# Seven accumulator banks as one set, freed in the order of their last readers, and two alternating orders of the attention step

## The chip, the cores and the metric

The kernel runs on one core of a Trainium2 chip. TensorE (PE) multiplies matrices and writes its results into PSUM, which has eight banks of 128 partitions by 512 fp32 values. VectorE (DVE), ScalarE (ACT) and GpSimd (POOL) do the rest; SyncE (SP) issues the transfers. Each engine takes its own instructions strictly in their order and waits on semaphores of the others. The metric is the device time of one launch in microseconds; lower is better.

## The reference

A transformer block on 2048 rows of 448 values, all in fp32: layer norm, attention with 16 heads of 28 values that share one key and one value head, output projection and residual; then layer norm, a gated feed-forward part of width 1792, and residual.

```python
q = (x @ wq).reshape(B, S, H, Dh).transpose(0, 2, 1, 3);  k = x @ wk;  v = x @ wv      # x = layernorm(A_x)
scores = jnp.einsum("bhqd,bkd->bhqk", q, k) * (Dh ** -0.5)
o = jnp.einsum("bhqk,bkd->bhqd", softmax(scores), v)
h = A_x + o.transpose(0, 2, 1, 3).reshape(B, S, H * Dh) @ wo
z = layernorm(h)
out = h + (silu(z @ w1) * (z @ w3)) @ w2
```

## The kernel before, in words

The rows are cut into four tiles of 512 (`t`), the heads into four groups of four (`g`). A **block** `i = 4t + g` is one tile with one group, so there are 16 blocks. Values that need fp32 precision are split into a high and a low part, and products are made of two or three fast passes.

**Opening stage.** Layer norm of all rows, transposes (`ln_tr`, L161), keys and values (`kv`, L405), queries of all blocks (`q`, L424). Between these the row maxima of block 0 and of the first quarter of block 1 are made in pairs (`both`, L231, called by `pairs`, L439).

**Attention stage.** Of each block the row maximum of all scores comes first, since the exponent must not overflow. It takes 64 **units** (`Unit`, L211): one matmul of 128 queries against 512 keys (L224) into a bank, and one maximum over 512 values on VectorE (`red`, L229). The exponents take 16 **steps** per block, one for each 128 keys (`c`): four **heads** (`Head`, L260), each of two accumulating matmuls (L271) into a bank and one Exp on ScalarE (L277), which writes to SBUF; then `pv` (L279), four matmuls side by side that add the step before to the output bank `po`. Step `s = 16 i + c`, 256 in all. The units run 20 steps ahead of the heads, four units in each of the first 236 steps (`a_units`, L337); the last 20 steps have heads alone.

Scores use half of the PE array's rows (64), so two matmuls on the two halves run side by side. I call such a couple a **slot**. A step of before is: heads 0 and 1 side by side (two slots); head 2 beside units u0 and u1 (two slots); `pv` of the step before; head 3 beside units u2 and u3 (two slots). This order is written out by hand in the loop from L547, the same for each step; `todo` (L505) adds other work at places `s + 0.4` (before the first two maxima), `s + 0.5` (after them, ahead of `pv`) and `s` (at the step's end).

That other work: at step 16i - 5 of block i the maxima are joined (`max_done`, L238); at step 16i - 3 they are transposed into a bank (`max_rows`, L242: PE L245, ScalarE copy L247) and their low part is made on VectorE (`max_low`, L250: L252), and eight small transfers on SP's queue (L258) put both parts into the rows that heads of block i use. Heads 0 and 1 of the block's first step need the fifth and the seventh of these. The output projection (`wo_rows`, L314) stands at the end of 12 even steps, the normalisation (`ln_norm`, L152) at the end of 8 odd steps, and the transposes for the feed-forward part (`ln_tr`) in 8 odd steps.

**Feed-forward stage.** For each tile 14 chunks of the width: `ffn1` (L594) makes two banks of 22 matmuls in all, `ffn2` (L606) adds 12 matmuls to four banks that stay taken for the whole tile.

**The banks.** Three banks (`ps_a`, tiles `pa`) serve the units, the projection and `ffn1`; four (`ps_b`, tiles `pb`) serve heads, queries, transposes and the feed-forward sums; one is `po`. Each set is handed out in a ring: a new tile takes the bank of the tile three (four) before it in the same set, and its first matmul waits until that tile's reader is done. In the heads-only steps one of the four heads uses a bank of `ps_a`.

Of the kernel before, what the change touches and what calls it, by code (L numbers as in the profile page):

```python
# [35 lines left out]
def block_kernel(  # L36
# [27 lines left out]
    dr_pool = ctx.enter_context(tc.tile_pool(name="dr", bufs=2, space=DRAM))  # L64
    ps_a = ctx.enter_context(tc.tile_pool(name="ps_a", bufs=3, space=PSUM))
    ps_b = ctx.enter_context(tc.tile_pool(name="ps_b", bufs=4, space=PSUM))
    ps_o = ctx.enter_context(tc.tile_pool(name="ps_o", bufs=1, space=PSUM))
# [30 lines left out]
    def put_late():  # L98
        for k in range(2):
            put_w13(10 + 2 * k, keep.tile([P, NG, T], F32, name=f"w13_{k}", tag=f"os{k}"))  # L100
            tl = keep.tile([P, NG, D], F32, name=f"w2_wo{k}", tag=f"wo{k}")
            for g in range(NG):
                W2[8 + 4 * k + g] = tl[:, g]


# [54 lines left out]

    def ln_tr(t, c, ps, spare=False):  # L161
        if c == 0:
            XT[t] = (xt_pool.tile([P, 4, T], F32R, name="xh"), xt_pool.tile([P, 3, T], F32R, name="xl"))
        xh, xl = XT[t]
        xns = LN[t][3]
        for n in range(NQ):
            pe.transpose(ps[:, n * P : (n + 1) * P], xns[n][:, c * P : (c + 1) * P], ident)  # L167
        se.activation(xh[:, c], ps, AF.Copy)
        eng = ve
        if spare:  # L170
            x32 = wk_pool.tile([P, T], F32, name="rb")
            se.activation(x32, ps, AF.Copy)
            eng, ps = ge, x32
        if c < 3:
            eng.tensor_tensor(xl[:, c], ps, f(xh[:, c]), op=ALU.subtract)  # L175
        else:
            eng.tensor_tensor(xh[64:128, 3], ps[64:128], f(xh[64:128, 3]), op=ALU.subtract)


    def a_bank():  # L180
        return ps_a.tile([P, T], F32, name="pa")

    def b_bank():
        return ps_b.tile([P, T], F32, name="pb")

# [25 lines left out]
    class Unit:  # L211
# [6 lines left out]

        def mm(self, bank=a_bank):
            i, n, kt, r = self.i, self.n, self.kt, rows(self.jj)  # L220
            if i not in MX:
                MX[i] = wk_pool.tile([P, 16, 4], F32, name="mx")
            self.ps = bank()
            pe.matmul(self.ps, QS[i][r, 2 * self.p, n * P : (n + 1) * P], KS[r, kt * T : (kt + 1) * T],  # L224
                      start=True, stop=True)

        def red(self):
            c = 8 * self.jj + 4 * self.p + self.n
            ve.tensor_reduce(MX[self.i][:, c, self.kt : self.kt + 1], self.ps, axis=AX.X, op=ALU.max)  # L229

    def both(i, p, n, kt, bank):  # L231
        us = [Unit(i, p, n, kt, jj) for jj in range(2)]
        for u in us:
            u.mm(bank)
        for u in us:
            u.red()
# [5 lines left out]
    def max_rows(i):  # L242

        ps = b_bank()
        pe.transpose(ps[:16, :P], NM[i], ident)  # L245
        mr = wk_pool.tile([16, 2, P], F32R, name="mr")
        se.activation(mr[:, 0], ps[:16, :P], AF.Copy)  # L247
        MR[i] = ps, mr

    def max_low(i):  # L250
        ps, mr = MR.pop(i)
        ve.tensor_tensor(mr[:, 1], ps[:16, :P], f(mr[:, 0]), op=ALU.subtract)  # L252
        for k in range(2):
            for jj in range(2):
                r = 64 * jj + 32 * k + 28
                for p in range(2):
                    c = 8 * jj + 4 * p
                    sy.dma_start(f(QS[i][r : r + 1, 2 * p]).rearrange("o (n q) -> o n q", n=NQ), f(mr[c : c + 4, k]))  # L258

    class Head:  # L260


        def __init__(self, i, c, j, bank=b_bank):
            self.i, self.c, self.j, self.bank = i, c, j, bank

        def mm(self, k):
            i, c, (p, jj) = self.i, self.c, divmod(self.j, 2)
            if k == 0:
                self.ps = self.bank()
            r = rows(jj)  # L270
            pe.matmul(self.ps, KS[r, c * P : (c + 1) * P], QS[i][r, 2 * p + k], start=(k == 0), stop=(k == 1))  # L271

        def exp(self):
            i, c, (p, jj) = self.i, self.c, divmod(self.j, 2)
            if jj == 0:
                PT[i, c, p] = p_pool.tile([P, 2, T], F32R, name="pt")
            se.activation(f(PT[i, c, p][:, jj]), self.ps, AF.Exp, bias=0.0, scale=SCALE)  # L277

    def pv(i, c):  # L279
# [33 lines left out]

    def wo_rows(t, n, bank=a_bank):  # L314
        ps = bank()[:, :D]
        k = 0
        for a, b in ((0, 0), (1, 0), (0, 1)):
            for g in range(NG):
                pe.matmul(ps, OS[a][:, g, n * P : (n + 1) * P], WO[b][:, g],  # L319
                          start=(k == 0), stop=(k == 11))  # L320
                k += 1
        ve.tensor_tensor(X[t][:, n], ps, X[t][:, n], op=ALU.add)

    def split_w(k):
# [12 lines left out]
    def a_units(step):  # L337
# [4 lines left out]
        p, n = divmod(c // 2, NQ)  # L342
        return [Unit(i, p, n, 2 * (c % 2) + k, jj) for jj in (1, 0) for k in range(2)]

# [6 lines left out]
    with tc.tile_pool(name="start", bufs=1) as sp:  # L351
# [49 lines left out]
        def tr(t, *cs):  # L401
            for c in cs or range(4):
                ln_tr(t, c, b_bank())

        def kv(t, between=None):  # L405
            cols = slice(t * T, (t + 1) * T)
            ps = b_bank()
            mm_D(ps[:96], WKV, XT[t], slice(0, 96), slice(0, T), between)
# [4 lines left out]
            sy.dma_start(f(KS[64:128, cols]), f(KS[0:64, cols]))  # L413
            sy.dma_start(f(KS[28::32, cols]), ones)
            return vt

        def va(t, vt):
            ps = b_bank()
            for n in range(NQ):
                pe.transpose(ps[:, 32 * n : 32 * n + 32], vt[64:96, n * P : (n + 1) * P], ident[64:96, 64:96])  # L420
            ve.tensor_copy(VA[:, NQ * t : NQ * t + NQ, :DH],
                           ps[:, :P].rearrange("p (n r) -> p n r", n=NQ)[:, :, :DH])

        def q(t, g, between=None):  # L424
            ps = b_bank()
            mm_D(ps, [w[:, :, 4 * g : 4 * g + 4].rearrange("p c h r -> p c (h r)") for w in WQ],
# [3 lines left out]
            else:  # L430
                se.activation(QR[t][:, g], ps, AF.Copy)

        first = [(both, 0, *divmod(pn, NQ), kt) for kt in range(4) for pn in range(8)]
# [5 lines left out]
        def pairs(n=2):  # L439
            banks = [a_bank, b_bank] * n  # L440
            while n > 0 and first:
                fn, *args = first.pop(0)
                if fn is both:
                    fn(*args, banks.pop(0))
                    n -= 1
                else:
                    fn(*args)

# [75 lines left out]
    for t in range(NT - 1):  # L524
# [9 lines left out]
        for c in range(4):  # L534
            at(e + 33.5 + 2 * c, lambda t, c: ln_tr(t, c, b_bank(), True), t, c)
    for t in range(NT):
# [10 lines left out]
    for s in range(LAST):  # L547
# [4 lines left out]
        if s == LAST - 2:  # L552
            WS[0, 0] = split_w2(0)
        hs = [Head(i, c, j, b_bank if au or j < 3 else a_bank) for j in range(4)]
        for k in range(2):
            for h in hs[:2]:
                h.mm(k)
        for h in hs[:2]:
            h.exp()
        if au:  # L560
            for j in (2, 3):
                for k in range(2):
                    hs[j].mm(k)
                    au[2 * (j - 2) + k].mm()
                hs[j].exp()
                if j == 2:
                    run(s + 0.4)
                for u in au[2 * (j - 2) : 2 * (j - 2) + 2]:
                    u.red()
                if j == 2:  # L570
                    run(s + 0.5)
                    if prev is not None:
                        pv(*prev)
        else:
            for k in range(2):
                for h in hs[2:]:
                    h.mm(k)
            for h in hs[2:]:
                h.exp()
            run(s + 0.4)  # L580
# [13 lines left out]
    def ffn1(t, k, W):  # L594
        ps = [a_bank(), a_bank()]
        for m in range(2):
            mm_D(ps[m], [w[:, :, m] for w in W], XT[t], slice(0, P), slice(0, T))
        sg = f(p_pool.tile([P, 2, T], F32R, name="pt")[:, 0])
        se.activation(sg, ps[0], AF.Silu)  # L599
        ve.tensor_tensor(sg, ps[1], sg, op=ALU.mult)  # L600
        h = p_pool.tile([P, 2, T], F32R, name="pt")
        se.activation(h[:, 0], sg, AF.Copy)  # L602
# [3 lines left out]
    def ffn2(t, k, n):  # L606
        if n == 0 and k == 0:
            Y[t] = [b_bank() for _ in range(NQ)]
        hid, w2s = HID[t, k], WS[t, k]
# [4 lines left out]
    def y_out(t, n):  # L614
        ve.tensor_tensor(X[t][:, n], Y[t][n][:, :D], X[t][:, n], op=ALU.add)
        if t == NT - 1:
            sy.dma_start(ov[t][:, n], X[t][:, n])
# [20 lines left out]
    for t in (NT - 2, NT - 1):  # L638
        for n in range(NQ):
            on(t - 1, 1 + n, ln_norm, t, n)  # L640
        for c in range(4):
            on(t - 1, 5 + c, lambda t, c: ln_tr(t, c, a_bank()), t, c)

# [58 lines left out]
```

## Time and profile before

| what | us |
|---|---|
| median of 3 runs (1276.83 to 1280.04) | 1278.54 |
| the profiled execution | 1276.48 |
| its span, first to last instruction | 1274.7 |
| opening stage | 0 to about 104 |
| attention, steps with units | about 104 to 787 |
| attention, heads-only steps | to about 834 |
| feed-forward | about 834 to 1275 |

The profile's page gives each engine's busy time, the chain of work that ended last, and groups of instructions by line. In the timeline, a row is a run of like instructions: start, length, engine, line, operation, tiles, count, and in brackets how long the engine was idle before and what ended that. A matmul's length includes its way through the array, so two matmuls in a row overlap and their starts tell more than their lengths; PEld is the loading of weights ahead of a matmul.

### The profile page before, as it was taken

What the parts mean: (1) busy time and instruction counts of PE and PEld (TensorE: products, weight loads), DVE (VectorE), ACT (ScalarE), POOL (GpSimd) and SP (SyncE); (2) the same over time, 40 slices, a digit from 0 to 9 for tenths busy, and PEclk for the clock granted to TensorE, in tenths of its full rate; (3) what the DMA queues carried; (4) which work ended last, traced back from release to release, by engine and by line L of the source; (5) the groups of instructions that cost most, each with busy time, mean ns of one, the idle gap of its engine ahead of it and who ended that gap; (6) DMA issues with size and microseconds to landing.
All of it is one profiled execution on the core that took longest, in us unless ns stands there. A gap on an engine that the chain in (4) does not pass through costs nothing.

```text
span 1274.7 us, 19969 instructions
## 1 busy us (share of the span) xinstructions
PE 1257.3 (99%) x7596; PEld 800.2 (63%) x7596; DVE 860.1 (67%) x1480; ACT 664.0 (52%) x1255; POOL 324.3 (25%) x240
## 2 busy tenths in 40 slices
PE   6999999999999999999999999999999999999998
PEld 5655555545555455555555544378888888888887
DVE  7998999999798998898998896033433324333223
ACT  3316777787578877678777678931111211211111
POOL 3201011101102100112100101253456455545551
PEclk9999999999999999999999999999999999999999
DMA  6220103101103111103110101022100000000000
GB/s 186 60 45 2 35 32 76 43 10 35 43 2 75 43 22 23 43 2 75 43 33 12 42 2 43 10 78 80 30 1 30 1 1 30 1 1 30 1 1 29
DMA packets 37960, 43.08 MB, mean 34 GB/s; under 512 B 12056, under 2 KB 30680, under 8 KB 37864
## 3 DMA queue, kind: packets, MB, share of 16 engines
q1 hardware_dynamic: 37864, 41.81, 12.7%
q8 instruction: 60, 0.98, 0.3%
q14 instruction: 36, 0.29, 0.1%
HBM read 20.25 MB, written 3.80 MB: 19 GB/s over the span
## 4 chain that ended last, share of the span: by engine, by line
PE 96%; DVE 2%; issue 1%; POOL 0%; ACT 0%; DMA 0%; SPq 0%; ACTq 0%; POOLq 0%
PE pb L271 27%; PE pa L116 23%; PE po L283 20%; PE pb L611 11%; PE pa L224 8%; PE pb L116 4%; PE pa L319 3%; PE pb L167 1%; DVE mx L229 1%; PE pa L167 0%; DVE xl L175 0%; PE pb L245 0%; PE pb L224 0%; DVE xn L155 0%; DMA X<-in_A_x_dram 0%
## 5 line engine op out<-in xcount | busy, mean ns | idle before, releaser
L229 DVE TENSOR_REDUCE mx<-pa 128x1 f32<-128x512 f32 x998 | 621.5, 682 | 58.7 <-PE pb L271 32.2
L277 ACT ACTIVATE pt<-pb 128x512 f32<-128x512 f32 x1004 | 527.1, 598 | 169.8 <-PE pb L271 138.4
L271 PEld LDWEIGHTS pb<-qs,KS 64*128 64x128 f32 x2008 | 257.7, 184 | 256.6 <-issue 198.0
L271 PE MATMUL pb<-qs,KS 64*128 64x512 f32 x2008 | 417.1, 406 | 1.6 <-issue 0.8
L224 PE MATMUL pa<-KS,qs 64*128 64x512 f32 x998 | 368.8, 445 | 0.8 <-DVE mx L229 0.7
L283 PE MATMUL po<-pt,VA 128*32 128x512 f32 x2048 | 273.5, 605 | 0.0
L116 PE MATMUL pa<-xh,qs 128*128 128x512 f32 x896 | 235.9, 394 | 0.0
L116 PEld LDWEIGHTS pa<-xh,qs 128*128 128x128 f32 x896 | 167.6, 187 | 38.9 <-issue 0.8
L600 DVE TENSOR_TENSOR pt<-pa,pt 128x512 f32<-128x512 f32 x56 | 38.7, 692 | 223.3 <-PE pa L116 223.3
L224 PEld LDWEIGHTS pa<-KS,qs 64*128 64x128 f32 x998 | 162.9, 184 | 37.1 <-DVE mx L229 9.7
L611 PE MATMUL pb<-qst,pt 128*128 128x448 f32 x672 | 145.8, 366 | 0.0
L599 ACT ACTIVATE pt<-pa 128x512 f32<-128x512 f32 x56 | 33.5, 598 | 197.5 <-PE pa L116 197.5
L611 PEld LDWEIGHTS pb<-qst,pt 128*128 128x128 f32 x672 | 125.5, 188 | 12.7
L602 ACT ACTIVATE pt<-pt 128x512 fp32r<-128x512 f32 x56 | 35.4, 632 | 152.8 <-DVE pt L600 152.8
L195 POOL TENSOR_TENSOR qst<-QR,qst 128x512 fp32r<-128x512 f32 x15 | 19.3, 1285 | 333.1 <-ACT qst L194 332.9
L116 PE MATMUL pa<-xl,qs 128*128 128x512 f32 x336 | 96.4, 394 | 0.0
L283 PEld LDWEIGHTS po<-pt,VA 128*32 128x32 f32 x2048 | 40.7, 108 | 64.1 <-issue 60.7
L328 POOL TENSOR_TENSOR qs<-QR,qs 128x1024 fp32r<-128x1024 f32 x32 | 76.4, 2389 | 15.6 <-DVE qs L327 15.6
L116 PEld LDWEIGHTS pa<-xl,qs 128*128 128x128 f32 x336 | 62.9, 187 | 15.5
L307 POOL TENSOR_TENSOR OT<-OT,rb 128x512 f32<-128x512 f32 x16 | 20.7, 1292 | 201.4 <-DMA rb<-sd 68.5
L603 DVE TENSOR_TENSOR pt<-pt 128x512 fp32r<-128x512 f32 x56 | 40.2, 718 | 39.1 <-ACT pt L602 39.1
L334 POOL TENSOR_TENSOR qst<-w_wo,qst 128x448 fp32r<-128x448 f32 x24 | 35.3, 1469 | 93.9 <-DVE qst L333 93.9
(91 smaller groups left out, 692.8 us busy)
## 6 DMA issues: line engine op xcount, KB each, us to landing
qs<-qst SPq DMA_DIRECT2D x128, 128.0 KB
rb<-sd SPq DMA_DIRECT2D x64, 64.0 KB
QR<-in_B_w_dram SPq DMA_DIRECT2D x16, 192.0 KB
X<-in_A_x_dram SPq DMA_DIRECT2D x3, 896.0 KB
out_dram<-X SPq DMA_DIRECT2D x3, 896.0 KB
qs<-mr SPq DMA_DIRECT2D x128, 2.0 KB
w<-in_B_w_dram SPq DMA_DIRECT2D x8, 192.0 KB
w_wo<-in_B_w_dram SPq DMA_DIRECT2D x6, 224.0 KB
```

Of the source, the lines that this page charges most:

```text
L116: pe.matmul(ps, lhs[b][:, cb, lsl], rhs[a][:, ca, rsl], start=(k == 0), stop=(k == len(terms) - 1),)
L224: pe.matmul(self.ps, QS[i][r, 2 * self.p, n * P : (n + 1) * P], KS[r, kt * T : (kt + 1) * T], start=True, stop=True)
L229: ve.tensor_reduce(MX[self.i][:, c, self.kt : self.kt + 1], self.ps, axis=AX.X, op=ALU.max)
L271: pe.matmul(self.ps, KS[r, c * P : (c + 1) * P], QS[i][r, 2 * p + k], start=(k == 0), stop=(k == 1))
L277: se.activation(f(PT[i, c, p][:, jj]), self.ps, AF.Exp, bias=0.0, scale=SCALE)
L283: pe.matmul(PO[i][32 * j : 32 * j + 32], VA[:, c], f(PT[i, c, j // 2][:, j % 2]), start=(c == 0), stop=(c == NC - 1))
L319: pe.matmul(ps, OS[a][:, g, n * P : (n + 1) * P], WO[b][:, g], start=(k == 0), stop=(k == 11))
L328: ge.tensor_tensor(wl, W13[k], f(wh), op=ALU.subtract)
L600: ve.tensor_tensor(sg, ps[1], sg, op=ALU.mult)
L602: se.activation(h[:, 0], sg, AF.Copy)
L603: ve.tensor_tensor(h[:, 1], sg, f(h[:, 0]), op=ALU.subtract)
L611: pe.matmul(Y[t][n][:, :D], hid[a][:, n * P : (n + 1) * P], w2s[:, b, :D], start=(k == 0 and m == 0), stop=(k == NF - 1 and m == 2))
```

## The change

All seven banks beside `po` become one set. `bank()` hands out the bank that stands first in a list; `done()` puts a bank at the end of the list where its last reader is issued. So the n-th tile takes the bank that was given back as the (n-7)th, whatever kind of tile that was: the first matmul of a unit may now wait for ScalarE, that of a head for VectorE.

The steps with units have two orders. Even steps keep the order above. In odd steps heads 0 and 1 come first, then heads 3 and 2 side by side, then units u0 and u1 side by side in one slot, `pv`, and units u2 and u3 in one slot. (The four units of an odd step are listed anew, so that two that run side by side use different halves of the array.) The number of matmuls, maxima, exponents and transfers stays the same, and so does the place of the other work: `s + 0.4`, `s + 0.5` and `s`. Heads-only steps keep their order.

```diff
-    ps_a = ctx.enter_context(tc.tile_pool(name="ps_a", bufs=3, space=PSUM))
-    ps_b = ctx.enter_context(tc.tile_pool(name="ps_b", bufs=4, space=PSUM))
+    ps_w = ctx.enter_context(tc.tile_pool(name="ps_w", bufs=1, space=PSUM))
...
+    free, used = list(range(7)), {}
+
+    def bank(name="pb"):
+        k = free.pop(0)
+        ps = ps_w.tile([P, T], F32, name=name, tag=f"bank{k}")
+        used[id(ps)] = ps, k
+        return ps
+
+    def done(ps):
+        free.append(used.pop(id(ps))[1])
...
         def red(self):
             c = 8 * self.jj + 4 * self.p + self.n
             ve.tensor_reduce(MX[self.i][:, c, self.kt : self.kt + 1], self.ps, axis=AX.X, op=ALU.max)
+            done(self.ps)
...
             ve.tensor_tensor(mr[:, 1], ps[:16, :P], f(mr[:, 0]), op=ALU.subtract)
+        done(ps)
...
             se.activation(f(PT[i, c, p][:, jj]), self.ps, AF.Exp, bias=0.0, scale=SCALE)
+            done(self.ps)
...
-        return [Unit(i, p, n, 2 * (c % 2) + k, jj) for jj in (1, 0) for k in range(2)]
+        us = [Unit(i, p, n, 2 * (c % 2) + k, jj) for jj in (1, 0) for k in range(2)]
+        return us if c % 2 == 0 else [us[0], us[2], us[3], us[1]]
...
+        def pair(a, b):
+            for k in range(2):
+                a.mm(k)
+                b.mm(k)
+            a.exp()
+            b.exp()
+
+        def beside(h, us):
+            for k in range(2):
                 h.mm(k)
-        for h in hs[:2]:
+                us[k].mm()
             h.exp()
...
+        pair(hs[0], hs[1])
+        if au and c % 2 == 0:
+            beside(hs[2], au[:2])
+            run(s + 0.4)
+            red(au[:2])
+            run(s + 0.5)
+            if prev is not None:
+                pv(*prev)
+            beside(hs[3], au[2:])
+            red(au[2:])
+        elif au:
+            pair(hs[3], hs[2])
+            for u in au[:2]:
+                u.mm()
+            run(s + 0.4)
+            red(au[:2])
+            run(s + 0.5)
+            pv(*prev)
+            for u in au[2:]:
+                u.mm()
+            red(au[2:])
         else:
...
+            pair(hs[2], hs[3])
```

The other users of banks (`ln_tr`, `kv`, `va`, `q`, `both`, `wo_rows`, `ffn1`, `ffn2`, `y_out`) take theirs from `bank()` and give it back with `done()` after their last reader in the same way.

The first place is TensorE's queue in a step with units, in block 4. L271 is a head's matmul (`pb`), L224 a unit's (`pa`), L283 is `pv` (`po`); the words in brackets are the semaphores that it waits on. Before, from head 2's first slot to the last slot of the step:

```order
L271 MATMUL pb_2787<-qs_1621,KS_89 128x512 [waits Activation_49]
L224 MATMUL pa_2789<-KS_89,qs_2214 128x512 [waits DVE_49]
L271 MATMUL pb_2787<-qs_1621,KS_89 128x512
L224 MATMUL pa_2792<-KS_89,qs_2214 128x512 [waits DVE_49]
...
L271 MATMUL pb_2803<-qs_1621,KS_89 128x512
L224 MATMUL pa_2805<-KS_89,qs_2214 128x512 [waits DVE_49]
L271 MATMUL pb_2803<-qs_1621,KS_89 128x512
L224 MATMUL pa_2808<-KS_89,qs_2214 128x512 [waits DVE_49]
```

With the change, an odd step from heads 3 and 2 on (lines are those of the changed file: L280 is a head, L231 a unit, L293 `pv`):

```order
L280 MATMUL pb_3080<-qs_1618,KS_86 128x512 [waits DVE_49]
L280 MATMUL pb_3082<-qs_1618,KS_86 128x512 [waits DVE_49]
L280 MATMUL pb_3080<-qs_1618,KS_86 128x512
L280 MATMUL pb_3082<-qs_1618,KS_86 128x512
L231 MATMUL pa_3089<-KS_86,qs_2211 128x512 [waits Activation_49]
L231 MATMUL pa_3091<-KS_86,qs_2211 128x512 [waits DVE_49]
L293 MATMUL po_2799<-pt_3043,VA_87 32x512 x2
L293 MATMUL po_2799<-pt_3053,VA_87 32x512 x2
L231 MATMUL pa_3099<-KS_86,qs_2211 128x512 [waits DVE_49]
L231 MATMUL pa_3101<-KS_86,qs_2211 128x512 [waits Activation_49]
```

The units of the odd step stand two by two on either side of `pv`, all four heads stand ahead of them, and the waits have changed sides: units wait for ScalarE's semaphore too, heads for VectorE's.

The second place is the odd step 16i - 3 on TensorE's queue, where the maxima of a block are transposed (L253 in the changed file, L245 before):

```order
L231 MATMUL pa_3228<-KS_86,qs_2813 128x512 [waits Activation_49]
L231 MATMUL pa_3230<-KS_86,qs_2813 128x512 [waits DVE_49]
L253 MATMUL pb_3232<-ident_84,nm_3173 16x128 [waits DVE_49]
L293 MATMUL po_2799<-pt_3181,VA_87 32x512 x2
L293 MATMUL po_2799<-pt_3192,VA_87 32x512 x2
L231 MATMUL pa_3251<-KS_86,qs_2813 128x512 [waits Activation_49]
L231 MATMUL pa_3253<-KS_86,qs_2813 128x512 [waits Activation_49]
```

Before, the transpose waited for ScalarE and stood behind four slots (heads 0 and 1, then head 2 with two units); now it waits for VectorE and stands behind five, with all four heads of the step ahead of it. On ScalarE its copy (`mr`) stood behind three exponents of the step and now stands behind four; on VectorE its second reader stands behind the first two maxima, as before.

More of the change, by code (lines that the diff above doesn't have):

```diff
@@ L159, in block_kernel, with ln_tr @@
     XT = {}
-    def ln_tr(t, c, ps, spare=False):
+    def ln_tr(t, c, spare=False):
+        ps = last = bank()
         if c == 0:
@@ L177, in ln_tr @@
             eng.tensor_tensor(xh[64:128, 3], ps[64:128], f(xh[64:128, 3]), op=ALU.subtract)
[L180 to L184, printed above, removed]
+        done(last)
     MR = {}
@@ L217, in __init__, with mm @@
             self.i, self.p, self.n, self.kt, self.jj = i, p, n, kt, jj
-        def mm(self, bank=a_bank):
+        def mm(self):
             i, n, kt, r = self.i, self.n, self.kt, rows(self.jj)
@@ L222, in mm @@
                 MX[i] = wk_pool.tile([P, 16, 4], F32, name="mx")
-            self.ps = bank()
+            self.ps = bank("pa")
             pe.matmul(self.ps, QS[i][r, 2 * self.p, n * P : (n + 1) * P], KS[r, kt * T : (kt + 1) * T],
@@ L229, in red, with both @@
             ve.tensor_reduce(MX[self.i][:, c, self.kt : self.kt + 1], self.ps, axis=AX.X, op=ALU.max)
-    def both(i, p, n, kt, bank):
+            done(self.ps)
+    def both(i, p, n, kt):
         us = [Unit(i, p, n, kt, jj) for jj in range(2)]
         for u in us:
-            u.mm(bank)
+            u.mm()
         for u in us:
@@ L242, in max_rows @@
     def max_rows(i):
-        ps = b_bank()
+        ps = bank()
         pe.transpose(ps[:16, :P], NM[i], ident)
@@ L260, in block_kernel, with __init__ @@
     class Head:
-        def __init__(self, i, c, j, bank=b_bank):
-            self.i, self.c, self.j, self.bank = i, c, j, bank
+        def __init__(self, i, c, j):
+            self.i, self.c, self.j = i, c, j
         def mm(self, k):
@@ L268, in mm @@
             if k == 0:
-                self.ps = self.bank()
+                self.ps = bank()
             r = rows(jj)
@@ L274, in exp @@
             i, c, (p, jj) = self.i, self.c, divmod(self.j, 2)
-            if jj == 0:
+            if (i, c, p) not in PT:
                 PT[i, c, p] = p_pool.tile([P, 2, T], F32R, name="pt")
             se.activation(f(PT[i, c, p][:, jj]), self.ps, AF.Exp, bias=0.0, scale=SCALE)
+            done(self.ps)
     def pv(i, c):
@@ L312, in o_split, with wo_rows @@
         ge.tensor_tensor(OS[1][:, g], o, f(OS[0][:, g]), op=ALU.subtract)
-    def wo_rows(t, n, bank=a_bank):
-        ps = bank()[:, :D]
+    def wo_rows(t, n):
+        po = bank("pa")
+        ps = po[:, :D]
         k = 0
@@ L322, in wo_rows @@
         ve.tensor_tensor(X[t][:, n], ps, X[t][:, n], op=ALU.add)
+        done(po)
     def split_w(k):
@@ L402, in tr @@
             for c in cs or range(4):
-                ln_tr(t, c, b_bank())
+                ln_tr(t, c)
         def kv(t, between=None):
             cols = slice(t * T, (t + 1) * T)
-            ps = b_bank()
+            ps = bank()
             mm_D(ps[:96], WKV, XT[t], slice(0, 96), slice(0, T), between)
@@ L414, in kv @@
             sy.dma_start(f(KS[28::32, cols]), ones)
+            done(ps)
             return vt
         def va(t, vt):
-            ps = b_bank()
+            ps = bank()
             for n in range(NQ):
@@ L422, in va @@
                            ps[:, :P].rearrange("p (n r) -> p n r", n=NQ)[:, :, :DH])
+            done(ps)
         def q(t, g, between=None):
-            ps = b_bank()
+            ps = bank()
             mm_D(ps, [w[:, :, 4 * g : 4 * g + 4].rearrange("p c h r -> p c (h r)") for w in WQ],
@@ L431, in q @@
                 se.activation(QR[t][:, g], ps, AF.Copy)
+            done(ps)
         first = [(both, 0, *divmod(pn, NQ), kt) for kt in range(4) for pn in range(8)]
@@ L439, in pairs @@
         def pairs(n=2):
-            banks = [a_bank, b_bank] * n
             while n > 0 and first:
                 fn, *args = first.pop(0)
[L443 to L447, printed above, removed]
+                fn(*args)
+                n -= fn is both
         for n in range(NQ):
@@ L534, in block_kernel @@
         for c in range(4):
-            at(e + 33.5 + 2 * c, lambda t, c: ln_tr(t, c, b_bank(), True), t, c)
+            at(e + 33.5 + 2 * c, lambda t, c: ln_tr(t, c, True), t, c)
     for t in range(NT):
@@ L553, in block_kernel, with red @@
             WS[0, 0] = split_w2(0)
-        hs = [Head(i, c, j, b_bank if au or j < 3 else a_bank) for j in range(4)]
-        for k in range(2):
-            for h in hs[:2]:
+        hs = [Head(i, c, j) for j in range(4)]
+        def pair(a, b):
[6 more added lines that the diff above has]
+            for k in range(2):
                 h.mm(k)
-        for h in hs[:2]:
+                us[k].mm()
             h.exp()
[L560 to L573, printed above, removed]
-        else:
[L575 to L579, printed above, removed]
+        def red(us):
+            for u in us:
+                u.red()
+        pair(hs[0], hs[1])
[17 more added lines that the diff above has]
+            for u in au[2:]:
+                u.mm()
+            red(au[2:])
+        else:
+            pair(hs[2], hs[3])
             run(s + 0.4)
@@ L594, in ffn1 @@
     def ffn1(t, k, W):
-        ps = [a_bank(), a_bank()]
+        ps = [bank("pa"), bank("pa")]
         for m in range(2):
@@ L599, in ffn1 @@
         se.activation(sg, ps[0], AF.Silu)
+        done(ps[0])
         ve.tensor_tensor(sg, ps[1], sg, op=ALU.mult)
+        done(ps[1])
         h = p_pool.tile([P, 2, T], F32R, name="pt")
@@ L607, in ffn2 @@
         if n == 0 and k == 0:
-            Y[t] = [b_bank() for _ in range(NQ)]
+            Y[t] = [bank() for _ in range(NQ)]
         hid, w2s = HID[t, k], WS[t, k]
@@ L615, in y_out @@
         ve.tensor_tensor(X[t][:, n], Y[t][n][:, :D], X[t][:, n], op=ALU.add)
+        done(Y[t][n])
         if t == NT - 1:
@@ L641, in block_kernel @@
         for c in range(4):
-            on(t - 1, 5 + c, lambda t, c: ln_tr(t, c, a_bank()), t, c)
+            on(t - 1, 5 + c, lambda t, c: ln_tr(t, c), t, c)
     prev = None
```

## The prediction

> **What bounds the kernel now.** I read the profile's page first, then the busy times of stretches, then one step row by row.
>
> ```profile
> span 1274.7 us, 19969 instructions
> PE 1257.3 (99%) x7596; PEld 800.2 (63%) x7596; DVE 860.1 (67%) x1480; ACT 664.0 (52%) x1255; POOL 324.3 (25%) x240
> PE 96%; DVE 2%; issue 1%; POOL 0%; ACT 0%; DMA 0%; SPq 0%; ACTq 0%; POOLq 0%
> ```
>
> ```profile
> 45.00:99.00 54.00, 53.09 (x228) 31.68 (x228) 49.99 (x86) 10.85 (x20) 4.23 (x6) 1.00 0.20 43
> 240.00:290.00 50.00, 50.00 (x367) 25.57 (x367) 45.65 (x78) 39.33 (x77) 4.75 (x5) 1.00 0.20 43
> 880.00:960.00 80.00, 80.00 (x361) 67.23 (x360) 29.82 (x55) 12.90 (x21) 40.62 (x22) 1.00 0.17 54
> ```
>
> (Columns: length, busy PE, PEld, DVE, ACT, POOL with their counts, granted clock, DMA share, GB/s.) The chain is PE to 96%, and PE looks 100% busy in attention (240 to 290) as in the feed-forward part (880 to 960), at the full clock. Alike they are not: weights load for 84% of the time in the second (67.23 of 80) and 51% in the first. A matmul's length includes its way through the array and hides short stalls, so I read the starts in a regular step:
>
> ```profile
> 421.16 0.50 PE L224 MATMUL pa<-KS,qs 64*128 64x512 f32 x1
> 421.50 0.39 PE L224 MATMUL pa<-KS,qs 64*128 64x512 f32 x1
> 421.73 0.62 PE L271 MATMUL pb<-qs,KS 64*128 64x512 f32 x4
> 422.19 0.39 PE L224 MATMUL pa<-KS,qs 64*128 64x512 f32 x1
> 422.48 0.49 PE L224 MATMUL pa<-KS,qs 64*128 64x512 f32 x1
> 422.90 1.06 PE L283 MATMUL po<-pt,VA 128*32 128x512 f32 x8
> 423.89 0.49 PE L271 MATMUL pb<-qs,KS 64*128 64x512 f32 x1
> ```
>
> ```profile
> 421.73 2.48 DVE L229 TENSOR_REDUCE mx<-pa 128x1 f32<-128x512 f32 x4 [0.25 <-PE pa L224]
> 421.93 2.10 ACT L277 ACTIVATE pt<-pb 128x512 f32<-128x512 f32 x4 [0.65 <-PE pa L224]
> 422.47 0.18 PEld L224 LDWEIGHTS pa<-KS,qs 64*128 64x128 f32 x1
> ```
>
> From slot to slot it is 0.23 us (421.50, 421.73, two slots to 422.19). Then u1 comes at 422.48, 0.29 later, and `pv` 0.42 after it, a step of 2.73 (421.16 to 423.89). Why is u1 late? Units have three banks, so u1 needs the bank of u2 of the step before; its maximum began at 421.73, took 0.68 (L229's mean) and ended at 422.41. At 422.47 the weights load, and since nothing hides that load, u1's matmul takes 0.49 instead of 0.39: 0.10 more. The loop is u2, its maximum, u1, `pv`, next u2. What a step takes without it is read at the heads-only steps, which have four slots:
>
> ```profile
> 808.46 0.96 PE L271 MATMUL pb<-qs,KS 64*128 64x512 f32 x5
> 809.59 1.06 PE L283 MATMUL po<-pt,VA 128*32 128x512 f32 x8
> 810.59 0.96 PE L271 MATMUL pb<-qs,KS 64*128 64x512 f32 x5
> ```
>
> 2.13 for four slots and `pv`; two more slots of 0.23 make **2.59**. So 0.14 of 2.73 is the wait for a bank, in each of 236 steps: 33 us is the most that better banks can give there. The feed-forward part has no such gap, and its sums keep four banks as before, which leaves three in turn for `ffn1`: I cost it at nothing, covered by PE's own queue.
>
> **The change, part by part.** PE's work stays: six slots and one `pv` per step. What changes is who waits for whom. I walk one even and one odd step by hand, at no stall, from the first slot of the even step (0). Slots: heads 0, 1 at 0 and 0.23; head 2 with u0 0.47, u1 0.70; `pv` 1.02; head 3 with u2 2.13, u3 2.36; odd step (marked '): heads 0', 1' at 2.60, 2.83; 3', 2' at 3.06, 3.29; u0', u1' 3.53; `pv` 3.85; u2', u3' 4.96; next even step 5.19.
>
> Readers: four maxima take 2.48, so one starts (2.48 - 0.68) / 3 = 0.60 after the other; exponents (2.10 - 0.60) / 3 = 0.50. A maximum starts about 0.46 after its matmul (421.16 to 421.73, less 0.10 of load), an exponent 0.43 (421.50 to 421.93). Maxima then end: u0' 4.67, u1' 5.27, u2' 6.10, u3' 6.70, and, still queued in the next pair, u0 2.11, u1 2.71, u2 3.31, u3 3.91. Exponents end: heads 0, 1, 2 at 1.26, 1.76, 2.26; 3 at 3.39; 0', 1', 3', 2' at 3.89, 4.39, 4.89, 5.39. A bank given back at x is filled without loss from x + 0.15 (0.05 to the load, 0.10 of load). The seventh tile back gives:
>
> ```
> tile  needed  bank of  free+0.15   |  tile  needed  bank of  free+0.15
> h0'    2.60    h1       1.91       |  h1     5.19    h3'      5.04
> h1'    2.60    h2       2.41       |  h2     5.66    h2'      5.54
> h2'    3.06    u1       2.86       |  u1     5.89    u1'      5.42
> u0'    3.53    h3       3.54       |  h3     7.32    u2'      6.25
> u1'    3.53    u2       3.46       |  u2     7.32    u3'      6.85
> ```
>
> The others have over 0.5 to spare. One place is short, by 0.01; I take 0.02, so the pair lasts 5.21 instead of 5.47: 118 pairs by 0.26 = **-30.7**. Bounds: -33 (no wait), and for each 0.1 us that the reads come late some +0.1 a pair, +12.
>
> **Block ends (steps 16i - 5 to 16i), 14 with units.**
>
> ```profile
> 600.15 1.29 DVE L229 TENSOR_REDUCE mx<-pa 128x1 f32<-128x512 f32 x2 [0.25 <-PE pa L224]
> 601.48 0.22 DVE L240 TENSOR_REDUCE nm<-mx 128x16 f32<-128x64 f32 x1
> 601.61 3.76 DVE L229 TENSOR_REDUCE mx<-pa 128x1 f32<-128x512 f32 x6
> 604.05 0.28 PE L245 MATMUL pb<-ident,nm 128*16 128x128 f32 x1
> 605.05 0.25 ACT L247 ACTIVATE mr<-pb 16x128 fp32r<-16x128 f32 x1
> 605.33 5.14 SPq L258 DMA_DIRECT2D qs<-mr  x8
> 794.73 1.61 DMA qs<-mr
> ```
>
> `max_done` sets VectorE back by 0.25 (601.61 instead of 600.15 + 2 x 0.60 = 601.35). The backlog lasts into step 16i - 3: the banks of u1, u2 and u3 come 0.25 later, so head 2' waits 0.05, u1' another 0.13, and the transpose, which needs u3's bank (4.31) at 3.94, 0.37. Behind it on PE stand `pv` and everything after. Together 0.55; its own 0.21 (604.05 to `pv`) was paid before. Then the transfers: the copy L247 now stands behind four exponents (5.29), the first issue comes at 5.57, the seventh 3.9 later (eight in 5.14), and lands 1.61 after: 11.08, usable at 11.23. Head 1 of the block needs it at 5.19 + 0.55 + 0.21 + 5.19 = 11.14: 0.1 to 0.2 late. Per block end 0.70: 14 x 0.70 = **+9.8** (bounds 0 and 1.2 each: 0 to 17). The last block's wait in heads-only steps (the DMA row at 794.73) stays.
>
> **Other work inside steps.**
>
> ```profile
> L155 DVE TENSOR_SCALAR xn<-X,mv,rs 128x448 f32<-128x448 f32 x8 | 4.0, 505 | 0.0
> L172 ACT ACTIVATE rb<-pb 128x512 f32<-128x512 f32 x8 | 5.0, 630 | 0.0
> L168 ACT ACTIVATE xh<-pb 128x512 fp32r<-128x512 f32 x8 | 4.9, 616 | 0.0
> 317.50 2.64 PE pa L319 x12
> 859.36 2.44 PE pa L319 x12
> ```
>
> Eight pairs have a normalisation: VectorE then needs 8 x 0.60 + 0.5 = 5.3, over PE's 5.19. Eight have a chunk of `ln_tr`, with 0.63 + 0.62 more on ScalarE, whose bank is given back late. These 16 pairs gain little: I take back 0.25 each, **+4** (bounds 0 and +8). The projection's 12 matmuls take 2.64 in attention and 2.44 in the feed-forward part, the difference again a bank of the units: 12 x 0.20 = **-2.4**. In the opening stage VectorE idles 4.0 of 54 us (45 to 99); PE may now run seven banks ahead of it: **-1** (bounds -3 and +2, since queries then queue behind maxima).
>
> Sum: -30.7 + 9.8 + 4 - 2.4 - 1 = -20.3. The profiled execution took 1276.48 (span 1274.7), so it would be 1256.2; the median of the runs shown is 2.06 above it. **Predicted 1258.**
>
> **The rivals.** (1) *The floor is reached at block ends too* (VectorE and SP in time): -31 to -35, some 1246. For it: SP's transfers land in time today, if barely. Against: the walk gives u0' no margin. Chance 0.10.
>
> (2) *VectorE binds.* If maxima can't overlap, eight take 8 x 0.682 = 5.46 a pair, and the step stays at 2.73: 1278. Against: four in 2.48, which is 0.60 apart; the same engine, operation and bank. [...] Chance 0.04, with the case that banks were not the cause.
>
> (3) *Half the gain.* Reads come 0.1 late in each pair (a semaphore more, a queue a little longer): +12, 1270. For it: three margins are under 0.2. Chance 0.11.
>
> (4) *Slower: ScalarE holds the shared banks.* Four exponents stand in a row in an odd step, and heads 1 and 2 of the next even step need the banks of the last two. If exponents came 0.60 apart (their full length, L277's mean 598 ns) instead of 0.50, 3' would end 0.30 and 2' 0.40 later, the two heads would wait 0.15 and some 0.13, and the pair is back at 5.47 while block ends and normalisations still pay: 1278.5 + 9.8 + 4 - 3.4 = 1289. It decides from about 0.17 of wait per pair (20.3 / 118), exponents 0.57 apart. Against: 0.50 apart in rows of 3 and 4 throughout. Chance 0.05.
>
> **How the numbers follow.** Forecast 0.70 (1250 to 1266), rivals 0.10, 0.04, 0.11, 0.05. The range, 1247 to 1268, takes in the forecast's case, most of (1) and part of (3). A measurement here tells 0.3% (3.8 us) from no change. Faster by more: forecast, (1), (3) but for a little, 0.90; same 0.05; slower 0.05.
>
> **What would show it.** In the changed kernel's timeline, starts of `pv` should alternate by about 2.35 and 2.85 (even to odd, odd to even; 1.02 to 3.85 is 2.83, 3.85 to 6.21 is 2.36), sum 5.19 to 5.25. In the waits, L231 on DVE and ACT should be small at regular steps, and 0.3 to 0.4 at L253, fourteen times. A wait of heads on `qs<-mr` should appear in each block's first step. VectorE's gaps in the regular steps should shrink to some 0.2 a pair. The feed-forward stretch should last as long as before. The prediction is wrong if `pv`-to-`pv` pairs stay above 5.4, or if heads wait on ScalarE (L280 on L286) over 0.1 in each pair.

## The result

The changed kernel takes **1257.37 us** (median; 1256.14 to 1257.54) against 1278.22 beside it: a ratio of 0.9834, with a 95% interval of 0.9817 to 0.9851. The forecast was 1258, in a range of 1247 to 1268. The profiled span went from 1274.7 to 1255.7, 19.0 less where the sum had 20.3; the profiled execution of before, 1276.48, lay under its median.

The page of the changed kernel:

```profile
span 1255.7 us, 19960 instructions
PE 1235.7 (98%) x7596; PEld 768.0 (61%) x7596; DVE 860.8 (69%) x1480; ACT 660.9 (53%) x1255; POOL 324.3 (26%) x240
PE 91%; DVE 6%; issue 1%; DMA 1%; POOL 0%; SPq 0%; ACT 0%; POOLq 0%
```

The busy times tell almost nothing of it: VectorE did the same work (860.1 then, 860.8 now), and PE was and is "busy" nearly throughout. The starts tell it. Two regular steps in PE's timeline (L293 is `pv`, L231 a unit, L280 a head):

```profile
151.31 1.07 PE L293 MATMUL po<-pt,VA 128*32 128x512 f32 x8
153.10 0.39 PE L231 MATMUL pa<-KS,qs 64*128 64x512 f32 x1
153.33 0.39 PE L231 MATMUL pa<-KS,qs 64*128 64x512 f32 x1
153.66 1.06 PE L293 MATMUL po<-pt,VA 128*32 128x512 f32 x8
```

From the odd step's `pv` to the even step's it is 2.35. The units of the even step come at 153.10 and 153.33, 0.23 apart; the 0.29 of before and its unhidden load are gone. The other way, even to odd, is 2.85, as the rows of a block end show below. A pair is 5.20 instead of 5.47. The readers keep up, in the rows of VectorE and ScalarE for the same time:

```profile
151.41 5.10 DVE L236 TENSOR_REDUCE mx<-pa 128x1 f32<-128x512 f32 x8
150.23 2.59 ACT L286 ACTIVATE pt<-pb 128x512 f32<-128x512 f32 x5 [0.49 <-PE pa L231]
```

Eight maxima run in 5.10 with no idle time that the view shows, on average a new one each 0.63; five exponents each 0.50. VectorE is now occupied almost for the whole pair, yet PE doesn't wait for it in a regular step: with shorter maxima (below) the pair stays as it is.

Where the time went, by the starts of `pv` in both traces (us; the last column is what the prediction had for the same term):

```
place                                        before   after    change         predicted
opening stage, to the first pv               104.15   102.96   -1.2           -1
regular pair of steps                        5.47     5.20     -0.27 each     -0.26 each
block end, the pair with the transpose       5.68     5.71     +0.30 over a regular pair and its own 0.21   0.55
block end, first heads of the block          -        -        +0.27 to +0.72 at nine of 14   0.15 at all 14
pair with a projection                       8.16     8.02     -0.14 each     -0.46 each
pair with a normalisation                    5.56     5.50     -0.06 each     -0.01 each
pair with a chunk of ln_tr                   6.06     5.85     -0.21 each     -0.01 each
heads-only steps                             46.4     47.6     +1.2           0
feed-forward, from the last pv to the end    442.96   442.90   0              0
```

### The profile page after: what moved, and what is told of

It is laid out like the page before. It is cut to its first block, busy times and chain, and to the rows that moved or that the text cites. A ratio compares the mean times of both kernels' runs of the same rounds, so it can differ in the third digit from the quotient of the medians.

```text
span 1255.7 us, 19960 instructions
## 1 busy us (share of the span) xinstructions
PE 1235.7 (98%) x7596; PEld 768.0 (61%) x7596; DVE 860.8 (69%) x1480; ACT 660.9 (53%) x1255; POOL 324.3 (26%) x240
## 4 chain that ended last, share of the span: by engine, by line
PE 91%; DVE 6%; issue 1%; DMA 1%; POOL 0%; SPq 0%; ACT 0%; POOLq 0%
PE pa L127 23%; PE pb L280 21%; PE po L293 19%; PE pb L641 11%; PE pa L231 9%; DVE mx L236 5%; PE pb L127 4%; PE pa L330 3%; PE pb L179 1%; DMA qs<-mr 0%; PE pb L253 0%; DVE xn L166 0%; DVE nm L248 0%; SPq L267 0%; DMA X<-in_A_x_dram 0%
## 5 line engine op out<-in xcount | busy, mean ns | idle before, releaser
L236 DVE TENSOR_REDUCE mx<-pa 128x1 f32<-128x512 f32 x1024 | 635.9, 682 | 36.3 <-PE pa L231 14.8
L286 ACT ACTIVATE pt<-pb 128x512 f32<-128x512 f32 x1024 | 533.9, 601 | 153.9 <-PE pb L280 118.1
L280 PE MATMUL pb<-qs,KS 64*128 64x512 f32 x2048 | 358.2, 403 | 2.0 <-DMA qs<-mr 2.0
L280 PEld LDWEIGHTS pb<-qs,KS 64*128 64x128 f32 x2048 | 227.5, 185 | 159.8 <-DVE mx L236 80.5
L231 PE MATMUL pa<-KS,qs 64*128 64x512 f32 x1024 | 291.7, 441 | 0.9 <-ACT vt L425 0.9
L293 PE MATMUL po<-pt,VA 128*32 128x512 f32 x2048 | 274.4, 606 | 0.0
L231 PEld LDWEIGHTS pa<-KS,qs 64*128 64x128 f32 x1024 | 133.7, 184 | 130.8 <-DVE mx L236 86.8
L293 PEld LDWEIGHTS po<-pt,VA 128*32 128x32 f32 x2048 | 40.9, 108 | 78.6 <-issue 72.0
```

What stands on the lines that cost most here:

```text
L293: pe.matmul(PO[i][32 * j : 32 * j + 32], VA[:, c], f(PT[i, c, j // 2][:, j % 2]), start=(c == 0), stop=(c == NC - 1))
```

## The experiments

Each ratio compares a run with the kernel before on the same chip. The runs were made on several chips, on which the kernel before took 1277.46 to 1278.22; so differences in us to the changed kernel mean little under 1 us.

### One set of banks, the order of before

```diff
-        return us if c % 2 == 0 else [us[0], us[2], us[3], us[1]]
+        return us
...
-        if au and c % 2 == 0:
+        if au:
             beside(hs[2], au[:2])
...
-        elif au:
-            pair(hs[3], hs[2])
...
```

> The seven banks as one set, but every step in the order of before. Theory (the two parts need each other): unit u1 now takes the bank of head 3 of the step before. At the floor of 2.59 that head's exponent ends at 3.39 (counted from its step's start), usable at 3.54, and u1 wants it at 3.29: 0.25 late in every step, a step of 2.84 instead of 2.73. 236 steps make some +20 to +26: 1298, between 1288 and 1306, slower than before. Rival (a larger common set is the gain, the orders add little): 1250 to 1265.

Measured: 1299.78, a ratio of 1.0177 (1.0160 to 1.0194). Slower, as the theory had it. `pv` to `pv`, and the wait of u1's load for an exponent:

```profile
151.45 1.07 PE L293 MATMUL po<-pt,VA 128*32 128x512 f32 x8
153.86 0.18 PEld L231 LDWEIGHTS pa<-KS,qs 64*128 64x128 f32 x1 [0.20 <-ACT pt L286]
154.28 0.16 PEld L293 LDWEIGHTS po<-pt,VA 128*32 128x32 f32 x8 [0.24 <-issue]
```

The step is 2.83 (151.45 to 154.28), against 2.84 worked out by hand. More banks within reach make it slower, because the bank that comes up for u1 is the one of head 3, read last.

### The two orders, the banks of before

```diff
-    ps_w = ctx.enter_context(tc.tile_pool(name="ps_w", bufs=1, space=PSUM))
+    ps_a = ctx.enter_context(tc.tile_pool(name="ps_a", bufs=3, space=PSUM))
+    ps_b = ctx.enter_context(tc.tile_pool(name="ps_b", bufs=4, space=PSUM))
...
     def bank(name="pb"):
+        return (ps_a if name == "pa" else ps_b).tile([P, T], F32, name=name)
```

> The two alternating orders, but the banks of before (three for units, four for heads). Theory: head 2 of an odd step takes the bank of head 3 of the even one, wanted at 3.06 and usable at 3.54, and u1 of the even step takes that of u2 of the odd one, wanted at 5.89 and usable at 6.25: some 0.5 to 0.8 lost per pair against the floor of 5.19, so pairs of about 6.0 against 5.47 before; 118 pairs make +60: 1338, between 1315 and 1350. Rival (the orders carry the gain, the set is a detail): 1250 to 1270.

Measured: 1335.98, 1.046 (1.0444 to 1.0475). In PE's rows (L289 is `pv`, L276 a head, L227 a unit here):

```profile
149.92 1.07 PE L289 MATMUL po<-pt,VA 128*32 128x512 f32 x8
152.34 0.29 PEld L276 LDWEIGHTS pb<-qs,KS 64*128 64x128 f32 x3 [0.43 <-ACT pt L282]
155.51 0.18 PEld L227 LDWEIGHTS pa<-KS,qs 64*128 64x128 f32 x1 [0.29 <-DVE mx L232]
155.94 1.07 PE L289 MATMUL po<-pt,VA 128*32 128x512 f32 x8
```

A head waits for ScalarE in the odd step and a unit for VectorE in the even one, the two places that were named; the pair is 6.02 (149.92 to 155.94). Each part alone is slower than before. Together they are faster, since the orders make what the common set needs: banks whose readers finish in the order in which they are wanted.

### Short maxima in the kernel before, and in the changed one

```diff
-            ve.tensor_reduce(MX[self.i][:, c, self.kt : self.kt + 1], self.ps, axis=AX.X, op=ALU.max)
+            ve.tensor_reduce(MX[self.i][:, c, self.kt : self.kt + 1], self.ps[:, : T // 2], axis=AX.X, op=ALU.max)
```

> The kernel before, with each maximum over half of its 512 values (so the maxima of half of the keys are left out). Theory: the step of 2.73 is the loop through u2's maximum; a maximum shorter by some 0.26 frees the bank before u1 wants it, and the step falls to TensorE's own 2.59: 236 x 0.14 and a little at the projections, 1245, between 1240 and 1250. Rival (2.73 is TensorE's own time, or the turn to and from pv): within 4 us of before, 1274 to 1282.

> The changed kernel, with each maximum over half of its 512 values (so the maxima of half of the keys are left out). Theory: regular pairs are at TensorE's 5.20 and stay there; what goes is VectorE's part of the block ends (0.3 of 0.76 each) and of the eight normalisations (0.3 each): 4 to 8 us, 1251. Rival (VectorE is still what a pair waits for): pairs under 5.1 and 1240 or less.

Measured: 1242.90 in the kernel before, 0.9729 (0.9715 to 0.9744); 1251.82 in the changed one, 0.9800 (0.9786 to 0.9815). Kernel before with short maxima, its `pv`:

```profile
151.84 1.06 PE L283 MATMUL po<-pt,VA 128*32 128x512 f32 x8
154.42 1.06 PE L283 MATMUL po<-pt,VA 128*32 128x512 f32 x8
```

A step of 2.58: the step of before was held by the maximum and by nothing else, and PE's own time for a step is what the heads-only steps had told. The changed kernel with short maxima, around a block end:

```profile
171.39 1.07 PE L293 MATMUL po<-pt,VA 128*32 128x512 f32 x8
174.25 0.28 PE L253 MATMUL pb<-ident,nm 128*16 128x128 f32 x1
174.46 1.07 PE L293 MATMUL po<-pt,VA 128*32 128x512 f32 x8
176.93 1.06 PE L293 MATMUL po<-pt,VA 128*32 128x512 f32 x8
```

The step with the transpose takes 3.07 (171.39 to 174.46): a regular 2.85 and 0.21 of its own. The same place in the changed kernel, up to the first heads of the block:

```profile
174.47 1.06 PE L293 MATMUL po<-pt,VA 128*32 128x512 f32 x8
177.83 1.07 PE L293 MATMUL po<-pt,VA 128*32 128x512 f32 x8
180.18 1.06 PE L293 MATMUL po<-pt,VA 128*32 128x512 f32 x8
182.67 0.42 PE L231 MATMUL pa<-KS,qs 64*128 64x512 f32 x2
183.01 1.07 PE L293 MATMUL po<-pt,VA 128*32 128x512 f32 x8
185.81 0.64 PE L293 MATMUL po<-pt,VA 128*32 128x512 f32 x4
```

3.36, so the wait there is 0.30 and it is VectorE's backlog, since short maxima take it away. Not all of it is won: with short maxima the next interval is 2.47 (174.46 to 176.93) instead of 2.35 (177.83 to 180.18), so the two together gain 0.17; why was not tried. Regular pairs are 5.20 and 5.21, so PE is what a pair costs now. With short maxima the changed kernel is 9 us behind the old one. There the common set and the alternating order have no wait left to take away; their regular pairs are a little longer (5.21 against 5.18, some 4 us in all), and their block ends cost more: by the starts of `pv` the first heads of a block come late at 11 of 14 in both, by 6.7 us in all here and by 2.7 in the old kernel. In the changed kernel above, 183.01 to 185.81 is such a place: 2.80 where 2.35 is regular.

One view misleads here. Waits of the changed kernel, and below them of the same with short maxima:

```profile
PEld pa L231 <- DVE mx L236: 81.0, 98, 0.8
PEld pb L280 <- DVE mx L236: 80.5, 98, 0.8
```

```profile
PEld pb L280 <- DVE mx L236: 98.1, 117, 0.8
PEld pa L231 <- DVE mx L236: 80.5, 96, 0.8
```

By these, PE's weight loads wait for VectorE for 160 us, and longer where the maxima are short. They don't cost that: 0.8 is the time for which `pv` occupies PE while the next load stands behind it, idle anyway. In the kernel before the same 0.84 stands in the rows under "issue". My own list of signs (small waits of L231 on VectorE and ScalarE) would have been read wrongly from this view; the starts were the sign to go by.

### Transfers in the order of need

```diff
-        for k in range(2):
-            for jj in range(2):
-                r = 64 * jj + 32 * k + 28
-                for p in range(2):
-                    c = 8 * jj + 4 * p
+        for p, k, jj in ((0, 0, 0), (0, 0, 1), (0, 1, 0), (0, 1, 1), (1, 0, 0), (1, 1, 0), (1, 0, 1), (1, 1, 1)):
+            r, c = 64 * jj + 32 * k + 28, 8 * jj + 4 * p
```

> The changed kernel, with the eight small transfers of a block's maxima issued in the order in which the heads need them: both parts for head 0 and head 1 first, so that head 1 needs the fourth and no longer the seventh. Theory (the first heads of a block wait for the transfers): the fourth lands 1.9 us earlier, so the 0.3 to 0.7 in each of nine block ends goes (3.9 in all), and 1.9 of the last block's wait in the heads-only steps: -6, 1251, between 1249 and 1253. Rival (the long gap there is the bank of the transpose and its followers): no change, 1256 to 1259.

Measured: 1254.68, 0.9817 (0.9804 to 0.9830). That is 2.7 below the changed kernel, half of what was expected, and the intervals of the two overlap; the trace tells the rest. The interval at the first heads of block 2, by `pv` (L290 here), is 2.35:

```profile
183.11 1.06 PE L290 MATMUL po<-pt,VA 128*32 128x512 f32 x8
185.46 1.07 PE L290 MATMUL po<-pt,VA 128*32 128x512 f32 x8
```

So the waits at the block ends were the transfers, and they went (one of 0.16 was left): 3.7 less over the 14 block ends, as expected. The last block gained nothing (47.8 for the heads-only steps, after 47.6). In heads-only steps head 3 follows head 2 at once, with no `pv` between, so that the block's first step still needs the eighth transfer; I had left that out.

### The projection behind `pv`

```diff
-            at(e + 14 + 2 * n, wo_rows, t, n)
-            at(e + 14 + 2 * n, ln_stats, t, n)
+            at(e + 14 + 2 * n + 0.6, wo_rows, t, n)
+            at(e + 14 + 2 * n + 0.6, ln_stats, t, n)
...
                 pv(*prev)
+            run(s + 0.6)
             beside(hs[3], au[2:])
```

> The changed kernel, with the output projection moved from the end of its even step to right behind pv in the same step. Theory (the 0.37 that each of 12 projections costs beyond its 12 x 0.20 is TensorE turning from the two halves to the whole array and back): behind pv one of two turns falls together with pv's own, so 0.1 to 0.2 less each: -1 to -3, 1255.5. Rival (it is a wait for a bank, as the prediction had it): the bank is free there for longer, so all 0.37 go: -4.4 and more, 1253 or less. A third: the turn costs the same everywhere: 1257.

Measured: 1265.91, 0.9904 (0.9891 to 0.9918): 8.5 more than the changed kernel. No theory had that sign. First the projection in the changed kernel (L330, then the next step's heads), then in this one:

```profile
317.06 0.39 PE L231 MATMUL pa<-KS,qs 64*128 64x512 f32 x1
317.38 2.71 PE L330 MATMUL pa<-WO,OS 128*128 128x448 f32 x12
320.01 1.20 PE L280 MATMUL pb<-qs,KS 64*128 64x512 f32 x8
```

```profile
317.88 2.70 PE L330 MATMUL pa<-WO,OS 128*128 128x448 f32 x12
320.51 0.18 PEld L280 LDWEIGHTS pb<-qs,KS 64*128 64x128 f32 x1 [0.30 <-issue]
320.62 0.62 DVE L333 TENSOR_TENSOR X<-pa,X 128x448 f32<-128x448 f32 x1 [2.07 <-PE pa L330]
321.27 0.63 DVE L155 BATCH_NORM_STATS2 st<-X 128x6 f32<-128x448 f32 x1
322.75 0.18 PEld L231 LDWEIGHTS pa<-KS,qs 64*128 64x128 f32 x1 [0.64 <-DVE mx L236]
```

A pair with a projection in the changed kernel costs 2.81 more than a regular one, where twelve matmuls alone are 2.43 (2.64 and 2.44 were the two rows of before). Part of this is seen in the first fence: the projection begins 0.32 after the last slot, 0.23 being regular, and the next heads come 2.63 after it. Behind `pv` the first of these falls away: 317.88 to 320.51 is 2.63 in all, 0.18 less than 2.81. But the two operations on VectorE that follow it (0.62 and 0.63) now stand ahead of the maxima of u2 and u3, which were still to come, and the odd step's u1 waits for u2's bank: 0.64, and 0.10 of unhidden load. In all the interval with a projection is 6.29 instead of 5.66, at each of the 12. So one turn less saves what the first theory said, and moving the projection costs more.

That no bank is waited for at the projection is told by the kernel before itself:

```profile
317.12 0.39 PE L271 MATMUL pb<-qs,KS 64*128 64x512 f32 x1
317.44 2.70 PE L319 MATMUL pa<-WO,OS 128*128 128x448 f32 x12
320.07 0.95 PE L271 MATMUL pb<-qs,KS 64*128 64x512 f32 x5
```

Again 0.32 from the last slot and 2.63 to the next heads. All twelve projections show 0.32 or 0.33 and 2.62 to 2.67 in both kernels, with full maxima as with short ones.

This edit was also run together with the transfers in the order of need. Expected, before either had been measured, were the two gains added up, 1249.5 (1247 to 1252), against 1253 or more if one gives back what the other gains. Measured: 1261.98, 0.9876 (0.9859 to 0.9892). The two did add up, but one of them is a loss: the run is 3.9 below the one with the projection moved alone (their intervals just touch), and its intervals with a projection are 6.29 there too.

### The transpose one step earlier

```diff
-        at(NC * i - 2.6, max_rows, i)
-        at(NC * i - 2.5, max_low, i)
+        at(NC * i - 4, max_rows, i)
+        at(NC * i - 2.6, max_low, i)
```

> The changed kernel, with the transpose of a block's maxima at the end of step 16i - 4 instead of inside step 16i - 3, its second reader at the first place of that step. Theory: its bank is free there (0.30 less per block end), the transfers start some 2 us earlier (the 3.9 of all block ends and 2 of the last block's wait go), but it stands alone between heads and pays two turns of TensorE, some 0.2 to 0.4 more each: -4.2 - 5.9 + 4.2 = -6, 1251, between 1249 and 1254. Rival (block ends wait for the maxima, wherever the transpose stands): 1256 to 1259.

Measured: 1253.78, 0.9812 (0.9799 to 0.9826), 3.6 below the changed kernel, with intervals that overlap, and just inside the theory's range. Its rows at a block end:

```profile
174.90 1.06 PE L293 MATMUL po<-pt,VA 128*32 128x512 f32 x8
176.24 0.39 PE L280 MATMUL pb<-qs,KS 64*128 64x512 f32 x1
176.56 0.28 PE L253 MATMUL pb<-ident,nm 128*16 128x128 f32 x1
176.77 1.27 PE L280 MATMUL pb<-qs,KS 64*128 64x512 f32 x8
177.80 0.76 PE L231 MATMUL pa<-KS,qs 64*128 64x512 f32 x2
178.06 0.18 PEld L231 LDWEIGHTS pa<-KS,qs 64*128 64x128 f32 x1 [0.30 <-DVE mx L236]
178.49 1.06 PE L293 MATMUL po<-pt,VA 128*32 128x512 f32 x8
```

3.59 instead of 3.36: the step costs 0.74 over a regular 2.85, 0.23 more than the transpose's own 0.21 and the wait of 0.30 together. But the wait has not gone: it moved to u1, whose weights load only after a maximum, so that `pv` comes 0.69 after u0 (177.80 to 178.49), not 0.34 as in a regular step (182.67 to 183.01 in the changed kernel above). That leaves some 0.4 for the transpose alone between heads, its own 0.21 and some 0.2 for the two turns, the least that the theory had. The block's first heads no longer wait (2.35), and the last block's wait, 3.5 in the changed kernel, is gone as well. Plus 14 x 0.23, minus 3.9 and 3.5: -4.2.

### The transpose behind `pv`, with the transfers in the order of need

```diff
-        at(NC * i - 2.6, max_rows, i)
-        at(NC * i - 2.5, max_low, i)
+        last = i == NI - 1
+        at(NC * i - 4 if last else NC * i - 3 + 0.6, max_rows, i)
+        at(NC * i - 2.6 if last else NC * i - 3, max_low, i)
...
             pv(*prev)
+            run(s + 0.6)
             for u in au[2:]:
```

> The changed kernel with the transfers in the order of need, and the transpose of a block's maxima behind pv of step 16i - 3 instead of ahead of it (its second reader at that step's end); for the last block alone the transpose at the end of step 236, as in the run that moved all of them there. Theory (what is left at a block end is the wait of the transpose for u3's bank, 0.30, since with short maxima the same place took its own 0.21 alone): behind pv that bank is free since 0.6, and no turn of TensorE is added, so 14 x 0.30 go; the transfers start 0.2 to 0.3 later, which their new order has to spare; the last block's wait of 3.5 goes as it did there. 1254.7 - 4.2 - 3.5 = 1247, between 1245 and 1250. Rival (the wait moves on to the units behind pv, or the later copy makes the block's first heads wait again): 1251 or more.

Measured: 1253.25, 0.9809 (0.9796 to 0.9823), outside the theory's range. The rival holds for the block ends:

```profile
177.96 1.07 PE L290 MATMUL po<-pt,VA 128*32 128x512 f32 x8
179.70 1.29 DVE L236 TENSOR_REDUCE mx<-pa 128x1 f32<-128x512 f32 x2 [0.42 <-PE pa L231]
180.44 0.18 PEld L231 LDWEIGHTS pa<-KS,qs 64*128 64x128 f32 x1 [0.29 <-DVE mx L236]
180.87 1.06 PE L290 MATMUL po<-pt,VA 128*32 128x512 f32 x8
```

Behind `pv` the transpose waits for no bank, but it puts off u2 and u3, VectorE runs dry for 0.42, and u1 of the next even step waits for it: 2.91 where 2.35 is regular. The wait moved by one step, and both intervals together (2.98 and 2.91, against 3.36 and 2.35) cost 0.18 more than in the changed kernel. What this run gained is the last block's wait and the transfers'.

### Transfers in the order of need, and the last block's transpose earlier

```diff
-        at(NC * i - 2.6, max_rows, i)
+        at(NC * i - (4 if i == NI - 1 else 2.6), max_rows, i)
```

(and the transfers' order from above)

> The changed kernel with the transfers of a block's maxima in the order of need, and the last block's transpose alone moved to the end of step 236. Theory (the two waits for transfers lie in different places and add up): 3.9 at the block ends as in the run with the order of need, 3.6 at the last block as in the run with all transposes earlier, from the changed kernel's 1257.4: 1250, between 1248.5 and 1252. Rival (what one gives the other takes back): 1253 or more.

Measured: **1251.20**, 0.9795 (0.9781 to 0.9808), within the expected range and with an interval just clear of the changed kernel's; of the kernels that compute everything it is the fastest here. The chain of waits of the changed kernel at the last block, and of this one, shows what went:

```profile
775.60 1.61 DMA qs<-mr
777.25 1.90 PE pb L280 x7
```

```profile
772.20 1.37 PE pb L277 x8
774.57 1.14 PE pb L277 x8
```

Of the heads' wait for the last transfer nothing is left but 0.23 (1.37 instead of 1.14).

## Why the prediction was right, point by point

**What bounds the kernel** was read rightly. PE's 100% hid a loop through u2's maximum and three banks; with short maxima the same kernel ran at 2.59 per step, the floor taken from the heads-only steps.

**The regular pair** came out at 5.20 where the walk had 5.19 and I took 5.21. That needed the spacing of the readers (0.60 and 0.50), not their length. Rival (2) took the length of 0.682, by which eight maxima need 5.46; the changed kernel shows eight in 5.10, so it fell. Rival (3), reads 0.1 late in each pair, fell with the 5.20 as well, and rival (1) with the block ends, which did cost their share.

**The two parts.** The walk also gave the right times for each part alone, with the same rows and the same kind of rule (the seventh bank back in one set, the third or fourth back in two): 2.84 a step with one set alone, about 6.0 a pair with the orders alone. Rival (4), a set whose banks ScalarE holds, is just what one set without the second order shows, at 1300; with both orders exponents stayed 0.50 apart and it did not come about.

**Block ends**, +9.8 in the sum, made 8.1 (14 x 0.30 = 4.2 and 3.9 of transfers). The sum held, its two parts did not. The wait of the transpose and the units ahead of it is 0.30 instead of 0.55, so the wait from the backlog behind `max_done` was overstated. Both runs that moved the transpose found a wait for a maximum again, before a unit. The transfers came 0.27 to 0.72 late instead of 0.15, at nine block ends only: where a projection's 2.81 or a chunk of `ln_tr` lies before the first heads, nothing is late. The heads-only steps, with the last block's wait that I said would stay, grew by 1.2. Why its transpose comes later relative to the heads was not tried by itself.

**The projection**, -2.4, is the step that failed. I took 2.64 against 2.44 as a wait for a bank, and no bank is waited for: the starts around the projection are the same before and after, with full and with short maxima. Pairs with a projection cost 2.81 to 2.83 over a regular one in the changed kernel and in both kernels with short maxima, as worked out from the starts of `pv`. What stands there is PE's change from two halves to the whole array and back; that this is the cause is argued from the place of the extra 0.37 and from the 0.18 saved behind `pv`, since no run leaves the turn out. The kernel before had 2.69, because its step after a projection, with VectorE caught up, did without the 0.14 of every other step. So there was less to gain: 12 x 0.14 instead of 12 x 0.46, and nearly 4 us missing.

**Normalisations and chunks**, 4 taken back, took 2.2: pairs of 5.50 and 5.85 instead of 5.56 and 6.06 before. **The opening stage**, -1, gave 1.2. **The feed-forward part**, at nothing, changed by 0.06.

The misses are of both signs and of 1 to 4 us each; that the total came within 1 us of the forecast owes something to that, and so to luck.

## What to carry to other kernels

Where a busy engine has a suspiciously regular step, take the step's floor from a stage that does the same work without the suspect, then walk the ring of buffers by hand: who gives back the buffer that is wanted next, and when. Giving all buffers to one set is no gain by itself; it helps when the work is ordered so that readers finish in the order in which buffers are wanted, and here each half of that made the kernel slower alone. Work of a second engine that follows a moved instruction moves with it in that engine's queue, and has to be priced there.

## What the hardware showed that was not expected

A turn of TensorE between matmuls on 64 rows and matmuls on 128 rows costs time at each end: 0.32 from the last slot to the projection instead of 0.23, and 2.81 for a projection in attention against 2.44 among matmuls of its own form. The Trainium skill (TensorEngine Tiling (Array Packing), "Key Properties") says that changing the tiling mode drains TensorE; the trace agrees as far as these delays stand where the matmuls change form, and behind `pv`, where one turn is shared, the projection took 2.63. A transpose alone between heads cost some 0.4 by itself, where 0.21 was its price just ahead of `pv`.
